# Joined q/k rest rows, score groups merged per half, and a mode preference in the order, on a TensorE-bound four-layer attention kernel

## The chip, the core and the metric

The kernel runs on one core of a Trainium2 chip. The metric is the device time of one execution in microseconds (us). Runs of one kernel spread by 3 to 17 us, so small differences are compared only between kernels that ran beside each other.

## The reference

Four residual layers run over 2048 rows of 576 values. Layers of kind A are local attention (32 heads of 18, a window of 8 with stride 2). Layers of kind B are a recurrence over 64 segments of 32 rows: each segment attends, with 32 heads of 128, over 8 memory rows and itself, and its first 8 output rows are the next memory.

```
for s in range(n_seg):                                   # layer B, cut
    h = concatenate([mem, x[:, s*32:(s+1)*32]])          # 8 + 32 rows of 576
    q, k, v = h @ Wq, h @ Wk, h @ Wv                     # 32 heads of 128
    p = softmax(mask(q @ k.T * 128**-0.5))
    o = (p @ v) @ Wo
    mem = o[:, :8]; outs.append(o[:, 8:])
x = x + A(layernorm(x)); x = x + B(layernorm(x))         # and both once more
```

## The kernel before

Both B layers run at once as two "lanes", the second five segments behind. So a step has 80 columns (two segments of 32, two memories of 8); the first and last five of the 69 steps have one lane. The A layers' tiles fill TensorE between. A small planner in Python lays out all operations at build time: each has an engine, a duration, a priority and buffers, and at each free moment the ready operation of lowest priority number is emitted. The order on the chip is fixed from then on.

```
# q and k of 3 heads (cut): ten matmuls a head, the fifth of each over the last 64 of 576 rows
for wi in range(2):
    for kc in range(4):
        matmul(pv[:, hh, wi, a:b], lhsT=wt[:, kc, h*P:(h+1)*P], rhs=hT[:, kc, a:b], start=(kc == 0), stop=False)
    matmul(pv[:, hh, wi, a:b], lhsT=wr[:, (h%16)*P:(h%16+1)*P], rhs=hT[:, 4 + h//16, a:b], start=False, stop=True)
...
# scores of 16 heads, called once with kind "m" (memory) and once with "x"
matmul(v, lhsT=ident4, rhs=msk, start=True)              # the mask, 128*128 tile
for l in lanes: for i in range(4): for c in range(4):    # 128*32 tiles, four side by side
    matmul(v[c*32:(c+1)*32, ...], lhsT=q, rhs=k)
...
# the planner's choice (cut)
while heap:
    it = heapq.heappop(heap); o = it[2]
    ...
    if all buffers of o are free:
        pick = o
        break
    skipped.append(it)
```

TensorE takes a tile shape per matmul; 128*128 is the whole array, 128*32 one of four column strips, 32*128 one of four row strips.

## Time and profile before

| | before |
|---|---|
| time, median of 3 runs | 2204.92 us (2199.17 to 2209.19) |
| span of the profiled run | 2198.3 us, TensorE clock 0.993 |
| TensorE matmul busy / weight loads busy | 95% / 79% |
| matmuls | 62,649 |
| largest groups | L818 and L820 (q and k), L974 (output projection), L864 (v) |

The page's first part gives busy time by engine, the fourth the chain of work that ended last. How the two are read together stands at the head of the prediction.

### The profile page before, as it was taken

To read this page: it belongs to the slowest core of one execution; us is meant where nothing else is said; L and a number is where in the kernel's file an instruction comes from. 1 tells how busy PE (TensorE), PEld (TensorE's weight loads), DVE (VectorE), ACT (ScalarE), POOL (GpSimd) and SP (SyncE) were. 2 spreads that over 40 slices of the span, in tenths; PEclk is the share of its full clock that TensorE was granted. 3 is DMA by queue.
4 is the path that set the end of the run, shared out by engine and by line. 5 is a ranking of instruction groups with operands and counts; after the bars stand their busy time and mean duration, and the time that the engine had idled before them with its cause. 6 is when DMAs were issued, how large, how long until landed. Compare 5 with 4: busy or idle time off the path is not lost.

```text
span 2198.3 us, 136770 instructions
## 1 busy us (share of the span) xinstructions
PE 2094.2 (95%) x62649; PEld 1746.3 (79%) x62649; DVE 1438.0 (65%) x3599; ACT 1189.0 (54%) x2855; POOL 853.9 (39%) x1263
## 2 busy tenths in 40 slices
PE   2689999999999999999999999999999999999998
PEld 2577888888888888888888888878878888888876
DVE  4467676666667666666766676667667666765665
ACT  2345565555556555555555565555555555655544
POOL 4144433443444344344434433443343344333230
PEclk9799999999999999999999999999999999999999
DMA  9754343343343334334433343443334333432210
GB/s 286 219 163 137 119 122 110 116 138 111 111 130 120 114 117 129 121 106 133 123 107 118 123 129 112 120 123 115 111 123 129 112 120 123 122 101 80 71 57 10
DMA packets 158578, 265.39 MB, mean 121 GB/s; under 512 B 23592, under 2 KB 90032, under 8 KB 158000
## 3 DMA queue, kind: packets, MB, share of 16 engines
q1 hardware_dynamic: 153168, 237.77, 35.2%
q0 software_dynamic: 4832, 18.88, 2.6%
q8 instruction: 489, 8.01, 1.5%
q14 instruction: 89, 0.73, 0.1%
HBM read 240.46 MB, written 16.12 MB: 117 GB/s over the span
## 4 chain that ended last, share of the span: by engine, by line
PE 87%; DMA 8%; DVE 2%; issue 1%; POOL 0%; ACT 0%; SPq 0%; POOLq 0%; ACTq 0%; DVEq 0%
PE r L818 28%; PE r L974 17%; PE r L864 14%; PE r L557 7%; PE r L820 7%; DMA ring<-strip 6%; PE r L909 3%; PE r L897 3%; PE r L950 2%; PE r L667 2%; PE r L458 2%; PE r L631 1%; PE r L606 1%; DMA ring<-in_A_wqkv_dram 1%; DMA wo<-in_A_wo_dram 1%
## 5 line engine op out<-in xcount | busy, mean ns | idle before, releaser
L818 PE MATMUL r<-hT,wq 128*128 128x80 bf16 (+1 forms) x8832 | 667.8, 199 | 4.4 <-ACT hT L268 2.8
L818 PE MATMUL r<-hT,wk 128*128 128x80 bf16 (+1 forms) x8832 | 666.0, 199 | 0.1
L268 ACT ACTIVATE qk<-r 128x480 bf16<-128x480 f32 (+3 forms) x714 | 379.5, 532 | 285.7 <-PE r L820 251.5
L818 PEld LDWEIGHTS <-wq 128*128 128x128 bf16 x8832 | 443.4, 99 | 57.8 <-issue 44.2
L818 PEld LDWEIGHTS <-wk 128*128 128x128 bf16 x8832 | 447.5, 100 | 0.2 <-issue 0.2
L974 PE MATMUL r<-OT,wo 128*128 128x80 bf16 (+1 forms) x11040 | 423.4, 199 | 22.7 <-issue 15.1
L820 PE MATMUL r<-hT,wk_r 128*128 128x80 bf16 (+1 forms) x2208 | 439.2, 199 | 0.2 <-issue 0.2
L820 PE MATMUL r<-hT,wq_r 128*128 128x80 bf16 (+1 forms) x2208 | 439.2, 199 | 0.0
L974 PEld LDWEIGHTS <-wo 128*128 128x128 bf16 x11040 | 398.3, 99 | 32.8 <-issue 30.0
L275 POOL TENSOR_TENSOR big<-qT,kT 128x1024 bf16<-128x1024 bf16 x189 | 319.1, 1691 | 213.4 <-ACT kT L268 206.7
L864 PE MATMUL r<-wv,hT 128*32 128x512 bf16 x5376 | 351.9, 380 | 1.4 <-issue 1.4
L275 POOL TENSOR_TENSOR ex<-ex,sum 128x384 bf16<-128x384 bf16 x137 | 120.3, 878 | 557.3 <-ACT qk L268 396.9
L864 PEld LDWEIGHTS <-hT 128*32 128x32 bf16 x6720 | 166.5, 96 | 134.8 <-issue 2.2
L755 DVE TENSOR_REDUCE nmx<-r 128x4 f32<-128x320 f32 (+1 forms) x276 | 143.5, 520 | 184.3 <-PE r L909 183.1
L268 ACT ACTIVATE V<-r 128x512 bf16<-128x512 f32 x302 | 180.2, 597 | 114.8 <-PE r L864 106.4
L557 PE MATMUL r<-xn,ring 128*128 128x64 bf16 x4725 | 192.8, 194 | 28.9 <-DMA ring<-in_A_wqkv_dram 17.3
L820 PEld LDWEIGHTS <-wq_r 128*128 128x128 bf16 x2208 | 219.8, 100 | 0.0
L820 PEld LDWEIGHTS <-wk_r 128*128 128x128 bf16 x2208 | 219.7, 100 | 0.0
L557 PEld LDWEIGHTS <-ring 128*128 128x128 bf16 x4725 | 159.8, 98 | 45.9 <-DMA ring<-in_A_wqkv_dram 18.2
L270 DVE CAST big<-r 128x256 bf16<-128x256 f32 x255 | 112.9, 484 | 93.7 <-PE r L631 92.8
L275 POOL TENSOR_TENSOR big<-big 128x640 bf16<-128x640 bf16 (+1 forms) x34 | 50.0, 1470 | 315.5 <-DVE big L275 315.4
L268 ACT ACTIVATE OT<-r 128x320 bf16<-128x320 f32 (+1 forms) x350 | 125.9, 421 | 54.8 <-PE r L950 54.3
(148 smaller groups left out, 3186.3 us busy)
## 6 DMA issues: line engine op xcount, KB each, us to landing
ring<-strip SPq DMA_DIRECT2D x488, 320.0 KB, 3.4
ring<-strip SPq DMA_DIRECT2D x244, 160.0 KB, 4.0
x1T<-x SPq DMA_DIRECT2D x32, 160.0 KB, 4.2
x<-x1T SPq DMA_DIRECT2D x32, 160.0 KB, 4.2
x3T<-x SPq DMA_DIRECT2D x32, 160.0 KB, 4.2
x<-x3T SPq DMA_DIRECT2D x32, 160.0 KB, 3.9
wo<-in_B_Wo_dram POOLq DMA_DIRECT2D x4, 1152.0 KB, 10.5
wq<-in_B_Wq_dram POOLq DMA_DIRECT2D x4, 1024.0 KB, 11.0
```

The lines of the kernel that those rows point to most:

```text
L268: nc.scalar.activation(out=out, in_=in_, func=ACT.Copy, scale=1.0 if scale is None else scale)
L270: (nc.vector if e == "DVE" else nc.gpsimd).tensor_copy(out=out, in_=in_)
L275: (self.nc.vector if e == "DVE" else self.nc.gpsimd).tensor_tensor(out=out, in0=in0, in1=in1, op=op)
L458: nc.tensor.matmul(psf, lhsT=(self.ones if c < 4 else self.ones_h)[:, :], rhs=xs.t[:, c].rearrange("p a t -> p (a t)"), start=(c == 0), st ...
L557: nc.tensor.matmul(ps.t[:, c * T:(c + 1) * T], lhsT=view()[:, kc, w0:w0 + P], rhs=xn.t[:, kc, :], start=(kc == 0), stop=(kc == 4))
L755: nc.vector.tensor_reduce(out=m, in_=v, axis=AX.X, op=ALU.max, negate=True)
L818: nc.tensor.matmul(pv[:, hh, wi, a:b], lhsT=wt[:, kc, h * P:(h + 1) * P], rhs=hT.t[:, kc, a:b], start=(kc == 0), stop=False)
L820: nc.tensor.matmul(pv[:, hh, wi, a:b], lhsT=wr[:, (h % 16) * P:(h % 16 + 1) * P], rhs=hT.t[:, 4 + h // 16, a:b], start=False, stop=True)
L864: nc.tensor.matmul(ps.t[c * 32:(c + 1) * 32, :], lhsT=l, rhs=w, start=(kc == 0), stop=(kc == 4))
L897: nc.tensor.matmul(v, lhsT=self.ident4[:], rhs=msk, start=True, stop=False, skip_group_check=True)
L909: nc.tensor.matmul(out, lhsT=q_, rhs=k_, start=False, stop=True, skip_group_check=True)
L974: nc.tensor.matmul(psY.t[:, mb * W80 + c0:mb * W80 + c1], lhsT=self.wo[:, w0:w0 + P], rhs=self.OT[:, h % 16 // 4 * 8 + h // 16 * 4 + h % 4 ...
```

## The change

Three things were meant. The last 64 input rows of q and of k become one matmul: their weights lie one above the other in 128 partitions, and the moving operand has, as it already had, the rest rows once in the upper and once in the lower half with zeros elsewhere (block-diagonal), so that 160 columns give q's and k's share. The memory and x scores of a half are one operation with both masks first, to change the tile shape less often. And the planner prefers an operation of the mode that TensorE is in. New priorities come with it.

```diff
+                        if alt is not None and o.prio > alt.prio + PR["w"]:
+                            skipped.append(it)
+                            break
 ...
-                            pick = o
-                            break
+                            if e != "PE" or o.mode == mode:
+                                pick = o
+                                break
+                            if alt is None:
+                                alt = o
 ...
-                    nc.tensor.matmul(pv[:, hh, wi, a:b], lhsT=wr[:, (h % 16) * P:(h % 16 + 1) * P],
-                                     rhs=hT.t[:, 4 + h // 16, a:b], start=False, stop=True)
+                nc.tensor.matmul(pv[:, hh, :, a:b], lhsT=self.Wb[0][1][:, h * P:(h + 1) * P], rhs=hT.t[:, 4:6, a:b],
+                                 start=False, stop=(hh == n - 1), skip_group_check=True)
 ...
-    def scores(self, t, r, kind, prio):
+    def scores(self, t, r, prio):
+            for v, msk in ((m, mask_m), (x, mask_x)):        # shortened here
+                nc.tensor.matmul(v, lhsT=self.ident4[:], rhs=msk, start=True, stop=False, skip_group_check=True)
+            # then 16 memory scores, then 16 a lane of x scores
 ...
-PR = dict(qk=0.218, qkd=0.046, v1=1.418, v0=1.316, m0=-0.184, x0=-0.028, m1=-0.12, x1=-0.059, ...
+PR = dict(qk=0.388, qkd=0.053, v1=1.358, v0=0.674, w=-0.059, s0=0.051, s1=-1.024, ...
```

More of the change, by code (lines that the diff above doesn't have):

```diff
@@ L153, in run @@
                     skipped = []
-                    pick = None
+                    pick = alt = None
                     held = set()
@@ L170, in run @@
                         if all(len(self.pools[p]) >= k and p not in held for p, k in need.items()):
-                            pick = o
-                            break
-                        if HOLD:
+                            if e != "PE" or o.mode == mode:
[3 more added lines that the diff above has]
+                                alt = o
+                        elif HOLD:
                             held.update(p for p, k in need.items() if k > 1 and len(self.pools[p]) < k)
@@ L177, in run @@
                         heapq.heappush(heap, it)
-                    if pick is None:
+                    if pick is None and alt is None:
                         continue
+                    pick = pick or alt
                     o = pick
@@ L336, in setup @@
         self.Wb = []
+        qkr = cp.tile([P, NH * P], BF16, name="wqk_r")
         for nm in ("wq", "wk", "wv"):
-            self.Wb.append((cp.tile([P, 4, NH * P], BF16, name=nm), cp.tile([P, (NH // 2) * P], BF16, name=nm + "_r")))
+            self.Wb.append((cp.tile([P, 4, NH * P], BF16, name=nm), cp.tile([P, (NH // 2) * P], BF16, name="wv_r") if nm == "wv" else qkr))
         self.wo = wo = cp.tile([P, NH * D + 64], BF16, name="wo")
@@ L416, in prologue @@
                 for hf in range(2):
-                    o = load(wr[hf * 64:(hf + 1) * 64, :], src[i][512:576, hf * 16:(hf + 1) * 16].rearrange("p h e -> p (h e)"), 0.26)
+                    if i < 2:
+                        out, in_ = wr[i * 64:(i + 1) * 64, hf * 16 * P:(hf + 1) * 16 * P], src[i][512:576, hf * 16:(hf + 1) * 16]
+                    else:
+                        out, in_ = wr[hf * 64:(hf + 1) * 64, :], src[i][512:576, hf * 16:(hf + 1) * 16]
+                    o = load(out, in_.rearrange("p h e -> p (h e)"), 0.26)
             for n in range(4):
@@ L815, in mm @@
                 for wi in range(2):
-                    wt, wr = self.Wb[wi]
                     for kc in range(4):
-                        nc.tensor.matmul(pv[:, hh, wi, a:b], lhsT=wt[:, kc, h * P:(h + 1) * P], rhs=hT.t[:, kc, a:b],
-                                         start=(kc == 0), stop=False)
-                    nc.tensor.matmul(pv[:, hh, wi, a:b], lhsT=wr[:, (h % 16) * P:(h % 16 + 1) * P],
-                                     rhs=hT.t[:, 4 + h // 16, a:b], start=False, stop=True)
-        o = pl.op("PE", 0.0003 + (0.358 if b - a == W80 else 0.29) * n, mm, prio, [*self.x_in[t].values(), *self.mem_in[t]] + ([self.w_in[wi][n_] for wi in range(2) for n_ in
-                  {h // 8 for h in heads}] if t == 0 else []), acq=[ps, sb], uses=[hT], mm=10 * n)
+                        nc.tensor.matmul(pv[:, hh, wi, a:b], lhsT=self.Wb[wi][0][:, kc, h * P:(h + 1) * P], rhs=hT.t[:, kc, a:b],
+                                         start=(hh == 0 and wi == 0 and kc == 0), stop=False, skip_group_check=True)
+                nc.tensor.matmul(pv[:, hh, :, a:b], lhsT=self.Wb[0][1][:, h * P:(h + 1) * P], rhs=hT.t[:, 4:6, a:b],
+                                 start=False, stop=(hh == n - 1), skip_group_check=True)
+        o = pl.op("PE", 0.0003 + (0.356 if b - a == W80 else 0.275) * n, mm, prio, [*self.x_in[t].values(), *self.mem_in[t]] + ([self.w_in[wi][n_] for wi in range(2) for n_ in
+                  {h // 8 for h in heads}] if t == 0 else []), acq=[ps, sb], uses=[hT], mm=9 * n)
         if g == 0:
@@ L874, in scores, with vm, vx @@
         qkt = dict(self.qkt)
-        ps = pl.buf("r")
-        m = kind == "m"
-        e_ = pl.buf("e" + kind)
-        pt, after = (pl.buf("pt"), None) if m else self.PT[r]
+        psm, psx, em, ex, pt = pl.buf("r"), pl.buf("r"), pl.buf("em"), pl.buf("ex"), pl.buf("pt")
         k0 = 16 * (1 - t % 2)
         on = self.lanes(t)
-        self.e_[kind] = e_
-        def view(tile_):
-            return tile_[:, 0:320].rearrange("p (i k) -> p i k", i=4) if m else \
-                tile_[:, 0:384].rearrange("p (l i k) -> p l i k", l=2, i=4)
+        def vm(tile_):
+            return tile_[:, 0:320].rearrange("p (i k) -> p i k", i=4)
+        def vx(tile_):
+            return tile_[:, 0:384].rearrange("p (l i k) -> p l i k", l=2, i=4)
         def mm(e):
-            v = view(ps.t)
+            m, x = vm(psm.t), vx(psx.t)
             def q(h, a, n):
@@ L894, in k @@
                 return qkt[h // 3].t[:, h % 3, 1, a:a + n]
-            msk = self.mask_m[:].unsqueeze(1).to_broadcast([P, 4, W80]) if m else \
-                self.mask_x[:].unsqueeze(2).to_broadcast([P, 2, 4, 48])
-            nc.tensor.matmul(v, lhsT=self.ident4[:], rhs=msk, start=True, stop=False,
-                             skip_group_check=True)
-            for l in range(1 if m else 2):
-                if not m and not on[l]:
-                    continue
+            for v, msk in ((m, self.mask_m[:].unsqueeze(1).to_broadcast([P, 4, W80])),
+                           (x, self.mask_x[:].unsqueeze(2).to_broadcast([P, 2, 4, 48]))):
+                nc.tensor.matmul(v, lhsT=self.ident4[:], rhs=msk, start=True, stop=False, skip_group_check=True)
@@ L902, in mm @@
+            for i in range(4):
+                for c in range(4):
+                    h = heads[i][c]
+                    nc.tensor.matmul(m[c * 32:(c + 1) * 32, i, :], lhsT=q(h, MC, 32), rhs=k(h, 0, W80), start=False, stop=True,
+                                     skip_group_check=True)
+            for l in range(2):
                 for i in range(4):
-                    for c in range(4):
+                    for c in range(4 if on[l] else 0):
                         h = heads[i][c]
-                        if m:
-                            out, q_, k_ = v[c * 32:(c + 1) * 32, i, :], q(h, MC, 32), k(h, 0, W80)
-                        else:
-                            out, q_, k_ = v[c * 32:(c + 1) * 32, l, i, :], q(h, XC[l], 32), k(h, KX[l], 48)
-                        nc.tensor.matmul(out, lhsT=q_, rhs=k_, start=False, stop=True, skip_group_check=True)
@@ L910, in scores @@
-        o = pl.op("PE", 0.29 if m else 0.41 if all(on) else 0.29, mm, prio, [self.qk_ev[g] for g in gs], acq=[ps, e_], uses=[qkt[g] for g in gs], mode="C",
-                  mm=17 if m or not all(on) else 33)
-        if m:
-            o = self.softmax(t, ps, e_, 320, prio, o, "DVE", view, lambda x: x[:, :, 16:96], lambda x: x[:, :, k0:k0 + 96],
-                             lambda x: x[:, :, :, MC:MC + 32], 384, pt, True)
-        else:
-            def tout(x):
-                f = x[:, 0, 0, 0:1]
-                return bass.AP(f.tensor, f.offset, [list(f.ap[0]), [W80 + XC[1], 2], [3 * W80, 4], [W80, 2], [1, 32]])
-            o = self.softmax(t, ps, e_, 384, prio + 0.02, o, "POOL", view, lambda x: x[:, :, :, 16:64],
-                             lambda x: x[:, :, :, k0:k0 + 64].rearrange("p l i (b q) -> p l i b q", q=32), tout, 512, pt, False, after)
@@ L922, in scores @@
-        self.PT[r] = (pt, o)
+                        nc.tensor.matmul(x[c * 32:(c + 1) * 32, l, i, :], lhsT=q(h, XC[l], 32), rhs=k(h, KX[l], 48), start=False,
+                                         stop=True, skip_group_check=True)
+        o = pl.op("PE", 0.68 if all(on) else 0.56, mm, prio, [self.qk_ev[g] for g in gs], acq=[psm, psx, em, ex],
+                  uses=[qkt[g] for g in gs], mode="C", mm=50 if all(on) else 34)
+        a = self.softmax(t, psm, em, 320, prio, o, "DVE", vm, lambda x: x[:, :, 16:96], lambda x: x[:, :, k0:k0 + 96],
+                         lambda x: x[:, :, :, MC:MC + 32], 384, pt, True)
@@ L924, in vs, with tout @@
+        def tout(x):
+            f = x[:, 0, 0, 0:1]
+            return bass.AP(f.tensor, f.offset, [list(f.ap[0]), [W80 + XC[1], 2], [3 * W80, 4], [W80, 2], [1, 32]])
+        a = self.softmax(t, psx, ex, 384, prio + 0.02, o, "POOL", vx, lambda x: x[:, :, :, 16:64],
+                         lambda x: x[:, :, :, k0:k0 + 64].rearrange("p l i (b q) -> p l i b q", q=32), tout, 512, pt, False, a)
+        self.PT[r] = (pt, a)
     def vs(self, t):
@@ L1024, in b_step @@
         for r in range(2):
-            self.scores(t, r, "m", t + PR[f"m{r}"])
-            self.scores(t, r, "x", t + PR[f"x{r}"])
+            self.scores(t, r, t + PR[f"s{r}"])
         for r in range(2):
@@ L1075 @@
 DLY = 5
-PR = dict(qk=0.218, qkd=0.046, v1=1.418, v0=1.316, m0=-0.184, x0=-0.028, m1=-0.12, x1=-0.059, p0=1.154, p1=-0.868,
-          o=0.742, od=0.026, mo=0.874, xo=0.964, v2=2.065, a1=1.97, a1s=2.63, a2=0.983, a2s=2.137, fin=1.091,
-          res=-1.854, ring=-7.995, A=(0.197, 0.389, 1.2, 0.915, 0.033, 1.069, 0.267, 1.19))
+PR = dict(qk=0.388, qkd=0.053, v1=1.358, v0=0.674, w=-0.059, s0=0.051, s1=-1.024, p0=0.894, p1=-0.981, o=0.434,
+          od=0.001, mo=0.097, xo=1.092, v2=2.128, a1=2.228, a1s=1.274, a2=0.453, a2s=7.821, fin=6.362, res=-5.467,
+          ring=-6.659, A=(-0.104, 0.482, 0.742, 0.737, 0.843, -0.012, 0.929, 0.994))
 LEAD = 5
```

## The prediction

> **What bounds the kernel now.** I read the busy shares first, then the chain that ended last, then the waits of TensorE, then the timeline of a stretch in the middle.
>
> ```profile
> PE 2094.2 (95%) x62649; PEld 1746.3 (79%) x62649; DVE 1438.0 (65%) x3599; ACT 1189.0 (54%) x2855; POOL 853.9 (39%) x1263
> ...
> PE 87%; DMA 8%; DVE 2%; issue 1%; POOL 0%; ACT 0%; SPq 0%; POOLq 0%; ACTq 0%; DVEq 0%
> PE r L818 28%; PE r L974 17%; PE r L864 14%; PE r L557 7%; PE r L820 7%; DMA ring<-strip 6%; PE r L909 3%; PE r L897 3%; PE r L950 2%; PE r L667 2%; PE r L458 2%; PE r L631 1%; PE r L606 1%; DMA ring<-in_A_wqkv_dram 1%; DMA wo<-in_A_wo_dram 1%
> ```
>
> TensorE is the bound: 95% busy, 87% of the last chain, the next engine at 65%. Busy does not say what a matmul costs, since consecutive matmuls overlap (one "takes" 202 ns in the groups while the next begins 36 ns later). Costs must come from start to start. The waits that TensorE itself suffered are small:
>
> ```profile
> PE r L557 <- DMA ring<-in_A_wqkv_dram: 17.3, 4, 12.0
> PE r L974 <- issue: 15.1, 20, 2.3
> PE r L557 <- DMA ring<-strip: 11.1, 23, 1.7
> ```
>
> The first is the start-up, which the stretches show too: of the first 100 us TensorE is busy 44.54, from 1000 to 2000 us it is busy 985.11. "issue" is 20 halts in which nothing visible is waited for. In the instruction records they recur at one position modulo 256 instructions (drifting slowly from 178 to 124), about 1.4 us after a 16 KiB packet of the instruction queue has ended: TensorE has run past what was fetched. I count some 20 us of these.
>
> So time is TensorE's stream: the start-to-start intervals of 62,649 matmuls. In the timeline (start, duration):
>
> ```profile
> 1015.41 0.20 PE L820 MATMUL r<-hT,wk_r 128*128 128x80 bf16 x1
> 1015.45 0.31 PE L818 MATMUL r<-hT,wq 128*128 128x80 bf16 x4
> 1015.59 0.20 PE L820 MATMUL r<-hT,wq_r 128*128 128x80 bf16 x1
> 1015.62 0.31 PE L818 MATMUL r<-hT,wk 128*128 128x80 bf16 x4
> ...
> 1023.92 0.39 PE L864 MATMUL r<-wv_r,hT 128*32 128x512 bf16 x4
> 1024.24 0.31 PE L897 MATMUL r<-mask_m,ident 128*128 128x320 bf16 x1
> 1024.48 0.33 PE L909 MATMUL r<-qk 128*32 128x80 bf16 x16
> 1024.74 0.34 PE L897 MATMUL r<-mask_x,ident 128*128 128x384 bf16 x1
> 1025.01 0.38 PE L909 MATMUL r<-qk 128*32 128x48 bf16 x32
> 1025.32 0.90 PE L557 MATMUL r<-xn,ring 128*128 128x64 bf16 x25
> ```
>
> Five matmuls of 80 columns take 1015.45 to 1015.62: 0.18 us, 36 ns each. Their record starts give 35.8 ns. One score pair (both halves of 16 heads) changes the tile shape four times, mask (128*128) to scores (128*32) and back, and takes 1024.24 to 1025.32, 1.08 us.
>
> **What the Trainium skill says.** "TensorE: Matmul & The Clock Gate", section "Wait — 56ns, not 53.3ns?", gives a warm matmul N/2.4 + about 2.5 ns from start to start, and a floor near 25 ns. The trace agrees: 35.8 ns at N = 80 (formula 35.8), 29 at 64 (29.2), 56 at 128 (55.8), 25 at 40 columns. "TensorEngine Tiling (Array Packing)", section "Key Properties", says that changing the tiling mode drains TensorE. The trace agrees and gives the price: after an 80-column full-array matmul the next starts 36 ns later in the same shape and 132 to 134 later in another; after a 512-column 128*32 group 206 against 312; after the 320-column mask 232 to 239 against 136 by the formula. About 0.10 us per change, in each direction. "Runtime: NRT & Kernel Launch", section "Instruction fetch mechanics", has instructions refilled in blocks of 16 KiB, 256 instructions; the halts at one position modulo 256 agree, but they are not "mostly hidden" here.
>
> **The change, part by part.**
>
> *q and k rest rows.* Ten matmuls a head become nine: two of 80 columns become one of 160. The same columns stream, so only the fixed cost of one matmul goes: 2 x 35.8 - (160/2.4 + 2.5 = 69.2) = 2.5 ns, an estimate by the page's formula. There are 1888 such heads (59 steps of both lanes x 32): 4.7 us. In the ten one-lane steps 2 matmuls at 40 columns, at the floor (25 to 26 ns), become one of 80: 51.2 - 35.8 = 15.4 ns x 320 heads = 4.9 us. Together 9.6 us, not the 156 us which 2208 x 2 x 35.8 ns of L820 might suggest. 2208 weight loads go too; loading overlaps and is no bound at 79%.
>
> *Merged scores.* Both masks first, then both score blocks: one change into the score shape instead of two, and one out. That is 138 pairs x up to 2. Reading the two builds' TensorE orders, changes of shape fall from 1423 to 1156: mask to scores from 276 to 138, and scores to something of another shape from 206 to 40 (98 groups now run straight into a v pass of the same 128*32 shape, where 70 did). 267 x 0.10 = 26.7 us.
>
> *Preference for the current mode.* As built it does nothing. The constant w is -0.059, and candidates come in rising priority, so once a ready operation of another mode is kept as alternative, the next has a priority above it minus 0.059 and ends the search at once. Building the changed kernel with the preference taken out gives the same order on all five engines. What remains of that part is the new set of priorities, and that reorders everything.
>
> Stream total: 9.6 + 26.7 = 36 us. As a cross-check I priced every neighbouring pair of both orders with the median (or trimmed mean) start-to-start of the same kind of pair in the trace: 2057 us before, 2018 after, 39 less. All of it is TensorE time, on the path.
>
> *What the new order gives back.* The work between a producer on TensorE and its consumer shrinks in places. In every second step the first output projection now follows its attention-times-V block after only ten 64-column transposes, 0.58 us by those same prices; the trace shows 0.79 us from last such matmul through the ScalarE eviction (0.44 us) to the first projection. So 0.2 us x some 30 = 6 us come back. Second: before, memory scores were done some 0.5 us ahead of x scores; now both reach VectorE at once, so the x softmax starts about that much later. Measured from scores to the last transpose it took 5.6 to 6.2 us, the new gap is 6.6 to 6.8 us: just enough, or short by 0.1 us. I take 2 us for that. The gap from the last projection to the next step's q and k is as before (1.25 us).
>
> Sum: 2204.9 - 36 + 8 = 2177; with half of what the pricing of pairs finds beyond the two terms, and some chance that re-chosen priorities also trim existing waits, I put 2172.
>
> **The rivals.**
>
> *Instruction fetch becomes the wait.* A group of 50 score matmuls is 100 instructions in some 0.9 us. Against: the group lies beside v passes (27 ns per instruction), and nine matmuls a head stretch 18 instructions over 355 ns (19.8 ns each instead of 17.9). Summing 320-instruction stretches, the new order is no denser. If fetch halts doubled: 2190.
>
> *Softmax or PSUM becomes the wait.* A score group now needs two PSUM banks of eight and both exponent buffers at once, and the burst lands on VectorE together. If each half waited 0.3 us more (138 x 0.3 = 41 us), the whole gain would go: about 2210. Against: VectorE 65%, and the attention block of the first half comes over 11 us after its scores.
>
> *Everything lands, with fewer waits.* If also half of the roughly 2 us per 100 us of waits in the middle vanish: about 2150, past the 2% mark of 2160.8.
>
> **Range and chances.** The stream saving is firm within some 4 us, what the order gives back is uncertain by 15, and single runs of before spread by 10. Range 2150 to 2194. Faster by over 2%: 0.24; within 2%: 0.73; slower: 0.03.
>
> **What would show it.** Matmuls 62,649 to 60,441; a 160-column matmul 69 ns before its successor; mask_m to mask_x 136 ns and no scores between; a two-step period in the middle down from 63.8 us to about 62.8. Waits of TensorE for OT before L984 of 0.2 us every second step. I am wrong if the 160-column matmul, whose operand lies in two pieces, streams slower than one per column, if pt becomes a frequent releaser of TensorE, or if "issue" grows well past 20 us.

## The result, and the profile after

The changed kernel takes 2169.28 us (median of 4, 2168.33 to 2171.51) against 2207.06 for before beside it (the three runs above and one more). The ratio is 0.9835 (95% interval 0.9805 to 0.9864), a gain of less than 2%. A ratio is the mean time of one kernel's runs over that of the other's of the same rounds, so not quite the ratio of the medians quoted.

The same parts of the page for the changed kernel, engines and chain:

```profile
PE 2063.7 (95%) x60441; PEld 1727.7 (80%) x60441; DVE 1397.7 (64%) x3541; ACT 1157.2 (53%) x2838; POOL 939.7 (43%) x1338
...
PE 90%; DMA 5%; DVE 2%; issue 1%; ACT 1%; POOL 1%; SPq 0%; POOLq 0%; ACTq 0%; DVEq 0%
```

TensorE is the bound as before, at the same 95%, and its share of the chain has risen. The matmuls are the 60,441 expected. The shares alone would not tell that the kernel is faster.

TensorE's own waits (who waited for whom: total us, times, longest):

```profile
PE r L533 <- DMA x<-in_A_x_dram: 25.0, 1, 25.0
PE r L570 <- DMA ring<-in_A_wqkv_dram: 16.0, 8, 7.4
...
PE r L984 <- issue: 7.4, 20, 0.9
...
PE r L570 <- DMA ring<-strip: 2.4, 6, 0.6
```

The first line is new: one wait of 25 us for one small input load. The second is the start-up's, about as before (17.3); "issue" at the output projection is down from 15.1, though halts elsewhere make up for it (below). The last was 11.1 us before and is 2.4. One score group in the middle of the run, in the timeline (start, duration):

```profile
1011.44 0.39 PE L877 MATMUL r<-wv_r,hT 128*32 128x512 bf16 x4
1011.76 0.31 PE L909 MATMUL r<-mask_m,ident 128*128 128x320 bf16 x1
1011.91 0.33 PE L909 MATMUL r<-mask_x,ident 128*128 128x384 bf16 x1
1012.16 0.33 PE L913 MATMUL r<-qk 128*32 128x80 bf16 x16
1012.32 0.43 PE L919 MATMUL r<-qk 128*32 128x48 bf16 x32
1012.57 1.06 PE L877 MATMUL r<-wv,hT 128*32 128x512 bf16 x16
```

From the first mask to what follows it is 0.81 us where it was 1.08. Those 1.08 us ended in one more change of shape, though. The like of it before is a group that a v pass followed:

```profile
1015.80 0.30 PE L897 MATMUL r<-mask_m,ident 128*128 128x320 bf16 x1
1016.03 0.33 PE L909 MATMUL r<-qk 128*32 128x80 bf16 x16
1016.29 0.34 PE L897 MATMUL r<-mask_x,ident 128*128 128x384 bf16 x1
1016.56 0.38 PE L909 MATMUL r<-qk 128*32 128x48 bf16 x32
1016.78 1.06 PE L864 MATMUL r<-wv,hT 128*32 128x512 bf16 x16
```

It took 0.98 us, so merging alone saves 0.17 here, two changes of shape. In the changed kernel the second mask starts 0.15 us after the first, no drain between, and the v pass after the scores has their shape, so nothing is drained there either, as in the group just shown.

To see where the time went I cut the run at the first output projection of steps 15 and 55, and sorted the start-to-start intervals of all matmuls in the middle stretch. An interval more than 60 ns above the median of its kind of pair counts as a "wait" if the matmul or its weight load carries a semaphore wait, and as a "halt" if not; "rest" is the stream. A short wait that recurs at the same pair stays in the rest.

| us | first matmul to step 15 | step 15 to 55 | of it halts | waits | rest | step 55 to last matmul |
|---|---|---|---|---|---|---|
| before | 542.0 | 1274.8 | 14.3 | 12.2 | 1248.4 | 367.7 |
| after | 540.3 | 1250.5 | 15.0 | 1.0 | 1234.5 | 363.2 |
| change | -1.7 | -24.3 | +0.7 | -11.2 | -13.9 | -4.5 |

So of 30.5 us in these two traces, 24.3 came in the middle 40 steps, a little more than half of it as a shorter stream and nearly half as waits that are gone. The first 15 steps gave almost nothing. The waits went with the new order: the same count gives 17.6 us of them in e6_before_qk below, which keeps the old order, and 0.7 to 2.2 us in the ten traces that have the new one (all but e5_pref and e7_oldprio). No run has the new order with the operations of before, so what the new priorities do without the merging is not known.

### The profile page after: what moved, and what is told of

Same layout as the page of the kernel before. It is cut to its first block, busy times and chain, and to the rows that moved or that the text cites. A ratio compares the mean times of both kernels' runs of the same rounds, so it can differ in the third digit from the quotient of the medians.

```text
span 2167.8 us, 132202 instructions
## 1 busy us (share of the span) xinstructions
PE 2063.7 (95%) x60441; PEld 1727.7 (80%) x60441; DVE 1397.7 (64%) x3541; ACT 1157.2 (53%) x2838; POOL 939.7 (43%) x1338
## 4 chain that ended last, share of the span: by engine, by line
PE 90%; DMA 5%; DVE 2%; issue 1%; ACT 1%; POOL 1%; SPq 0%; POOLq 0%; ACTq 0%; DVEq 0%
PE r L830 27%; PE r L984 18%; PE r L877 17%; PE r L570 7%; PE r L833 6%; PE r L960 3%; PE r L680 2%; PE r L909 2%; DMA ring<-strip 2%; PE r L471 2%; DMA ring<-in_A_wqkv_dram 2%; PE r L913 2%; PE r L644 1%; PE r L919 1%; PE r L619 1%
## 5 line engine op out<-in xcount | busy, mean ns | idle before, releaser
L830 PEld LDWEIGHTS <-wq 128*128 128x128 bf16 x8832 | 500.7, 98 | 31.6 <-issue 21.5
L833 PE MATMUL r<-hT,wqk_r 128*128 128x160 bf16 (+1 forms) x2208 | 507.9, 230 | 0.1
L275 ACT ACTIVATE qk<-r 128x480 bf16<-128x480 f32 (+3 forms) x635 | 333.2, 525 | 238.0 <-PE r L833 225.0
L282 POOL TENSOR_TENSOR big<-qT,kT 128x1024 bf16<-128x1024 bf16 x186 | 310.1, 1686 | 32.7 <-ACT kT L275 21.5
L282 POOL TENSOR_TENSOR big<-big 128x640 bf16<-128x640 bf16 (+1 forms) x59 | 117.6, 1994 | 414.7 <-ACT xs L465 245.0
L833 PEld LDWEIGHTS <-wqk_r 128*128 128x128 bf16 x2208 | 219.5, 99 | 0.2 <-issue 0.2
L570 PEld LDWEIGHTS <-ring 128*128 128x128 bf16 x4725 | 160.9, 98 | 42.7 <-DMA ring<-in_A_wqkv_dram 17.6
L275 ACT ACTIVATE OT<-r 128x320 bf16<-128x320 f32 (+1 forms) x377 | 138.3, 425 | 103.6 <-PE r L960 103.3
L275 ACT ACTIVATE big<-r 128x384 bf16<-128x384 f32 (+1 forms) x290 | 110.3, 443 | 92.8 <-issue 67.6
L769 DVE TENSOR_TENSOR r<-r,nmx 128x320 f32<-128x320 f32 (+1 forms) x276 | 147.1, 533 | 9.4
L877 PE MATMUL r<-wv_r,hT 128*32 128x512 bf16 x1344 | 133.2, 379 | 0.0
```

The lines of the kernel that those rows point to most:

```text
L275: nc.scalar.activation(out=out, in_=in_, func=ACT.Copy, scale=1.0 if scale is None else scale)
L282: (self.nc.vector if e == "DVE" else self.nc.gpsimd).tensor_tensor(out=out, in0=in0, in1=in1, op=op)
L570: nc.tensor.matmul(ps.t[:, c * T:(c + 1) * T], lhsT=view()[:, kc, w0:w0 + P], rhs=xn.t[:, kc, :], start=(kc == 0), stop=(kc == 4))
L769: nc.vector.tensor_tensor(out=v, in0=v, in1=m.unsqueeze(len(shp) - 1).to_broadcast(shp), op=ALU.add)
L830: nc.tensor.matmul(pv[:, hh, wi, a:b], lhsT=self.Wb[wi][0][:, kc, h * P:(h + 1) * P], rhs=hT.t[:, kc, a:b], start=(hh == 0 and wi == 0 and ...
L833: nc.tensor.matmul(pv[:, hh, :, a:b], lhsT=self.Wb[0][1][:, h * P:(h + 1) * P], rhs=hT.t[:, 4:6, a:b], start=False, stop=(hh == n - 1), sk ...
```

## The experiments

Each kernel is the changed one with the edit shown, unless it says before. "Rest", "halts" and "waits" are those of the table, in the middle 40 steps of the profiled run. The four kernels from a0_after to e3_tiled ran beside each other, so did e4_x1early to e7_oldprio, and so did a1_after to e9_cond_x1.

**a0_after and a1_after: the controls.** No edit.

> The changed kernel again, as the control for the three runs beside it: 2169 us as on record, ratio to before 0.9835. Nothing is tested by it alone.

> The changed kernel again, control for the three runs beside it: 2170 to 2172 us.

Measured: 2171.56 us (ratio 0.9812) and 2175.59 us (0.9829). The rest is 1234.5 us in both and in the trace on record, the same to 0.1 us, while halts run from 15.0 to 17.0 and the time up to step 15 from 540.3 to 549.2. So the stream repeats exactly, and what differs between runs of one kernel lies in halts and the start-up.

**e1_split: the join undone, the order kept.**

```diff
-                nc.tensor.matmul(pv[:, hh, :, a:b], lhsT=..., rhs=hT.t[:, 4:6, a:b], ...)
+                for wi in range(2):
+                    nc.tensor.matmul(pv[:, hh, wi, a:b], lhsT=..., rhs=hT.t[:, 4 + wi, a:b], ...)
```

> The changed kernel with the joined rest-row matmul taken apart again into two (80 columns each, or 40), the order of every engine left as it is. My theory (only the fixed 2.5 ns of a matmul goes in the wide steps, 15 ns a head in the one-lane steps): 9.6 us slower than the control, so about 2179. Rival: the join was worth nothing, because the operand in two pieces costs the 2.5 ns again (the records show 71.6 ns to the next matmul, not 69.2): about 5 us slower, from the one-lane steps alone. Rival: fewer instructions also spared fetch halts: 15 us or more slower, with issue waits of TensorE clearly up.

Measured: 2183.96 us (0.987), 12.4 above its control. The rest rises by 3.0 us (1237.5), which over the 1280 heads of the stretch is 2.3 ns a head; halts are 15.5 against 16.8. So the join is worth what was worked out, some 2.3 x 1888 = 4.4 us in the wide steps and about 5 in the one-lane ones; the remaining 3 us of the 12.4 have no cause shown; single runs of either kernel spread by 3.5 to 8. The record that alarmed me, 71.6 ns from a joined matmul to the next, is undone by its neighbours: the other 80-column intervals in the same heads average 35.5 ns in place of 35.8. A single interval was a bad witness, the sum over a head a good one. The fetch rival (15 us or more, with more halts) falls: 4416 instructions more brought no more halts in this stretch.

**e2_apart: the x mask back between the score blocks, all else in place.**

```diff
-  mask_m, mask_x, memory scores, x scores
+  mask_m, memory scores, mask_x, x scores
```

> The changed kernel with the same operations in the same order, but inside each of the 138 score groups the mask of the x scores is put back between the two score blocks: changes of tile shape go from 1156 to 1432. My theory (0.10 us a change, all on the path): 276 x 0.10 = 28 us slower than the control, about 2197. Rival (what the switches cost is hidden behind waits that follow): under 10 us slower. The memory scores are then ready earlier by about 0.35 us, which would show if the softmax were on the path.

Measured: 2193.08 us (0.991), 21.5 above its control. The rest rises by 14.2 us (1248.7) for 160 more changes of shape in the stretch: 0.089 us a change. So shape changes are on the path and nearly as dear as priced. 276 changes at 0.089 would be 24.6 us, where 21.5 was measured. Halts are 13.1 us, 3.7 fewer than in the control. A slower group may give the fetch more time, but that is not shown: the halts of other pairs with the same middle differ by as much (e8_tiled_x1).

**e3_tiled: masks as strips of the scores' own shape.**

```diff
-                nc.tensor.matmul(v, lhsT=self.ident4[:], rhs=msk, start=True, stop=False, skip_group_check=True)
+                for c in range(4):
+                    nc.tensor.matmul(v[c * 32:(c + 1) * 32], lhsT=self.ident4[:, c * 32:(c + 1) * 32], rhs=msk, start=True, ...)
```

> The changed kernel with each mask written by four 128*32 matmuls (one per column strip) in place of one 128*128, so that a score group is of one tile shape from its first instruction: shape changes from 1156 to 966, matmuls up by 828. My theory: 190 x 0.10 = 19 us faster than the control, about 2150, if four strips stream beside each other as the v passes do (206 ns for four of 512 columns). Rival: the strips go one after another, 2 x 3 more streams of 133 to 160 ns, and it is 40 us slower or worse. Rival: the group, now 112 instructions in a burst, brings fetch halts: gain under 8 us with issue waits up.

Measured: 2164.53 us (0.9782), 7.0 below its control. The same kind of place in its timeline:

```profile
1001.61 0.39 PE L877 MATMUL r<-wv_r,hT 128*32 128x512 bf16 x4
1001.83 0.31 PE L910 MATMUL r<-mask_m,ident 128*32 128x320 bf16 x4
1001.96 0.34 PE L910 MATMUL r<-mask_x,ident 128*32 128x384 bf16 x4
1002.13 0.32 PE L915 MATMUL r<-qk 128*32 128x80 bf16 x16
```

From the last v block to the memory scores it is 0.52 us, where the changed kernel has 1011.44 to 1012.16, 0.72. The strips do stream side by side (0.13 us to the next four), and the first rival falls. The rest is 13.1 us less for 120 fewer changes, 0.109 us each. But halts rise by 4.3 (21.1 against 16.8), which would fit the second rival; e8_tiled_x1 below puts that in doubt. The middle says -7.8 us in all, the time -7.0.

**e4_x1early and e4b_x1early: the second input tile's load first.** The line with the 25 us wait above has its cause in the queue of the SyncE transfers (start, duration):

```profile
10.04 0.35 SPq L443 DMA_DIRECT2D x<-in_B_mem_dram  x1
...
22.93 5.92 SPq L505 DMA_DIRECT2D wo<-in_A_wo_dram  x1
28.95 20.13 SPq L528 DMA_DIRECT2D x<-in_A_x_dram  x2
```

There is one buffer for input rows. The start memory takes it at 10 us, and the second tile's load, now of a lower rank, stands behind all the strips of A's weights, to be issued at 28.95 and to land some 19 us later among the B weights. Before, and again in e4b_x1early, it is issued at 10 us:

```profile
10.03 0.47 SPq L515 DMA_DIRECT2D x<-in_A_x_dram  x1
10.04 0.47 SPq L528 DMA_DIRECT2D x<-in_A_x_dram  x1
```

The edit:

```diff
-                      pr(0), [dep], acq=[x0])
+                      -2.6 if j == 1 else pr(0), [dep], acq=[x0])
```

> The changed kernel with one priority altered: the load of the second input tile goes ahead of the load of the start memory, as it did before the change; the steady order stays. My theory (the re-chosen priorities put that load behind the big weight loads, TensorE waited 25 us for it, and the first q and k came 17.7 us later, of which all but about 7 us was caught up within ten steps): first q and k at about 46 us again, and 7 us faster than the changed kernel, about 2162. Rival: nothing is caught up, 17 us faster. Rival: the start is bound by the weights anyway, within 2 us.

> The kernel of e4_x1early once more, now beside its control, since without one the gain read as anything from 8 to 13 us. Theory (late start, mostly caught up within ten steps): 7 to 10 us below the control. Rival (nothing caught up): 17 us below.

Measured: 2163.06 us (0.9777), and beside its control 2163.50 (0.9772), 12.1 below it, more than the 7 to 10 expected and less than 17. The first q and k start at 46.5 us (52.8 in the second trace) where the changed kernel has 63.6 and before 45.8. The expected 7 to 10 rested on one trace: there those 17.7 us of delay, set against before, had shrunk to 6.4 by step 5 and 0.6 by step 10. The two controls still had 8.8 and 12.0 at step 5, 5.2 and 8.7 at step 10. At step 15 the three traces of the changed kernel stand on average 2.7 us behind before (from 1.7 ahead to 7.1 behind), the two with the early load 6.0 and 7.1 ahead of it. So the late start is caught up in part only: about 9 us of it stay, in traces that differ by as much among themselves. Before, TensorE was busy only 44.54 of the first 100 us, so a late start has idle time to catch up in. So the new priorities brought a late start that costs the changed kernel about 12 us by the time measured, 9 by the traces.

**e5_pref: the preference turned on.**

```diff
-PR = dict(..., w=-0.059, ...
+PR = dict(..., w=0.3, ...
```

> The changed kernel with the preference for the current tile mode truly on (w = 0.3 in place of -0.059), all other priorities as they are: shape changes from 1156 to 1004. If switches alone counted: 152 x 0.10 = 15 us faster, about 2154. My theory: the order was chosen for w = -0.059, and work of one mode held together delays producers (attention blocks pushed to three in a row, then all projections), so TensorE waits more than it gains: 2160 to 2220, with PE waits for OT, pt or DMA up.

Measured: 2256.64 us (1.0208), some 85 us above the changed kernel, beyond my range. Shape changes are fewer (580 in the stretch against 680), waits 38.1 us against 1.0, and the start is longer too (571.7 us to step 15). For 88.7 us of that start the granted clock was at half, against 14 to 68 in the changed kernel's three traces, so a part of the longer start may be the clock. Of TensorE's waits over the whole run:

```profile
PE r L570 <- DMA ring<-strip: 16.8, 30, 1.1
PE r L728 <- DVE fin L1023: 12.7, 27, 0.6
```

The changed kernel had 2.4 and 0.4 us there. A preference that saves 0.1 us a time delays work whose consumers then wait. This shows what w = 0.3 does with priorities chosen without it, not that no preference could pay.

**e6_before_qk: before, with the join alone, its order kept.** The edit is the rest-row part of the diff of the change (the `matmul` lines), with the weight tile that it needs.

> The kernel before with only the joined rest-row matmul, its order on every engine kept (1423 shape changes). My theory: 9 to 10 us faster than before, ratio 0.9957. Rival: under 3 us, the join is hidden. Rival: over 20 us, because 4416 fewer TensorE instructions spare fetch halts.

Measured: 2197.55 us (0.9942, interval 0.9915 to 0.9968), 12.6 below before. The rest is 3.6 us less (1244.8), 2.8 ns a head. Its profiled run was the slowest of its six (2209.68). Together with e1_split: the join gives about 10 us in either order, 12.4 and 12.6 in time and 9.6 as worked out.

**e7_oldprio: the change with the priorities of before.**

```diff
-PR = dict(qk=0.388, ..., s0=0.051, s1=-1.024, ...
+PR = dict(qk=0.218, ..., s0=-0.184, s1=-0.12, ...
```

> The changed kernel with the priorities of before (score groups at the old priority of the memory scores): joined matmul and merged groups without the new priorities. Shape changes 975, fewer than the 1156 of the changed kernel, so by switches alone it should be 18 us faster than the changed kernel, about 2150. My theory: the priorities were chosen for another set of operations, waits come up in the middle (TensorE busy under 985 of 1000 us), and it is slower than the changed kernel: 2170 to 2230. What it is above 2170 is what the new priorities are worth.

Measured: 2443.05 us (1.1053), far beyond my range, although it changes shape less often than the changed kernel (560 times in the stretch against 680). Where TensorE waited:

```profile
PE r L570 <- DMA ring<-strip: 71.5, 82, 3.2
PE r L471 <- ACT xs L465: 44.7, 30, 1.5
PE r L984 <- ACT OT L275: 36.0, 68, 0.6
```

Waits in the stretch are 69.8 us, and the rest is up by 133, which holds short waits that recur, and slower matmuls: the granted clock from 600 to 1800 us is 0.95. The trace's clock records tell how: of the stretch's 1443.7 us, 140 were at half clock, some 7 us in every 72 (before and after had none there). In them 80-column matmuls followed each other after 66.7 ns in place of 35.6. That makes some 65 of the 133 us, an estimate from these figures. All four runs had 0.944 to 0.953, so it belongs to this kernel, but what brought the clock down is not shown. So join and merging together did not pay under the old priorities: 270 us slower than under the new ones, the clock's share included. How the two depend on each other in detail is not settled by this run.

**e8_tiled_x1: strips and the early load.** The edits of e3_tiled and e4_x1early.

> The early load of the second input tile together with the masks as 128*32 strips. If the two are independent: 7 (strips, as in e3_tiled) + 9 (load) = 16 us below the control, about 2155. Rival: less than 12, if the fetch halts that ate most of the strips' gain grow.

Measured: 2153.88 us (0.973), 21.7 below its control, where 16 were expected: 12.1 from the load and 9.6 from the strips on top of it. Rest 1221.4 as in e3_tiled, halts 17.5 where e3_tiled had 21.1. The order in the middle is the same in both; the start differs. So how many halts a kernel gets varies by some 4 us for reasons outside the burst itself, and the single figure of e3_tiled should not be leaned on.

**e9_cond_x1: strips only after a 128*32 block.**

```diff
+                        self.was = mode                                  # in the planner
 ...
+                if pl.was != "C":
+                    nc.tensor.matmul(v, lhsT=self.ident4[:], rhs=msk, start=True, ...)
+                    continue
```

> As e8_tiled_x1, but a group that follows a full-array matmul keeps its two full-array masks; only the 95 or so groups that follow a 128*32 block use strips. Shape changes as in e8_tiled_x1 (966), 258 matmuls fewer. If fetch halts are what took most of the strips' gain in e3_tiled, a shorter burst gives some back: 1 to 3 us below e8_tiled_x1, with issue waits down. If not: the same as e8_tiled_x1 within 1 us.

Measured: 2147.35 us (0.9704, interval 0.9691 to 0.9717), 28.2 below its control and 6.5 below e8_tiled_x1. This is the fastest kernel and correct; it beats before and after. Why it beats e8_tiled_x1 is open. The reason I gave is not borne out: halts in its profiled run are 22.2 against 17.5, the rest is the same 1221.4, and the two profiled runs differ by only 1.6 us (spans 2148.9 and 2150.5), while the timed medians differ by 6.5.

## Why the prediction was right

The predicted 2172 stands against 2169.28, inside the range of 2150 to 2194 and within 2%, to which it had given 0.73. The direction, the bound and the main mechanisms held. Not every term did. Of the signs it named, the matmul count and the two-step period came (63.7 to 62.5 us, where 62.8 was expected); the two short intervals came a little longer (71.6 ns after a 160-column matmul for 69, 143.5 from mask to mask for 136).

*Rest rows, 9.6 us.* Right: 2.3 to 2.8 ns a head in the wide steps by the rest of e1_split and e6_before_qk, where 2.5 was worked out; 12.4 and 12.6 us in time, some 3 us more than was worked out. (The 156 us of L820 that the prediction sets beside it should be 158; no sum uses it.)

*Merged scores, 26.7 us at 0.10 a change.* The mechanism is right, the size about a tenth too large. A change costs 0.089 us in e2_apart and 0.109 in e3_tiled, so 0.10 is fair for the stream. But in the middle 160 changes went (840 to 680) and the rest fell by 13.9 us, of which 3.0 belong to the join: 10.9 us, 0.068 each. Most of the difference is the give-back that the prediction counted apart: the 0.17 us of the next paragraph but one, which recur, sit in the rest. In this stretch there are 19 of them, 3.4 us; without them it is 14.3 us, 0.089 each, as in e2_apart. That other small differences between the two orders come to nothing is not shown: the pricing of pairs had 19.3 us for that stretch, join included, where 13.9 and 3.4 make 17.3.

*The preference does nothing.* Right, and lucky for the kernel: turned on with these priorities it costs 85 us.

*What the order gives back, 6 us for the projection.* Right in place: 26 times the first projection stands after the transposes (five of them turned out to be 128 columns wide, of finished rows) with an interval 0.17 us over its usual, 4.5 us in all; from attention block to projection it is 0.73 us where 0.58 was priced. *2 us for the later softmax*: wrong, nothing. TensorE waits for pt 5.8 us in six places in all, none of them from 600 to 1800 us.

*The rivals.* Fetch as the new wait: no, halts 14.3 to 15.0. Softmax or PSUM: no. Fewer waits: yes. I gave "half of the 2 us per 100 us" only as a rival that would end at 2150. That figure held halts too: waits and halts of the middle made 26.5 us before, 2.1 per 100 us, and 16.0 after, so 40% of it went, all of it waits (12.2 to 1.0).

*The halts.* That they recur at one position modulo 256 is right, and plainer than it was read. Counted over matmuls and weight loads alone, in order of start, the position does not drift: all 31 halts over 0.3 us of before (whole run) and all 39 of after stand at 193 to 195. The instruction queue moved 489 packets in before, and its 125,298 matmuls and weight loads over 256 are 489.4. So the fetch is well supported as their cause; no run changed it alone.

*What was missed.* The start: the new priorities moved one input load behind the weights, about 12 us by e4b_x1early. I had looked at the order of TensorE and not at that of the transfers, where one line would have shown it. The two missed terms, 11 us of waits gone and about 12 us at the start, nearly cancel. The closeness of the total owes something to that, and that much was luck.

## What to carry to other kernels

When one engine's stream is the bound, price it from start to start by kind of neighbour pair: joining two matmuls of 80 columns saved only some 2.5 ns, because the same columns stream, while a change of tile shape costs about 0.1 us here, as much as three matmuls of 80 columns. Look for instructions that could take the shape of their neighbours (the masks as strips gave 7.0 and 9.6 us). An order chosen for one set of operations has to be chosen anew when they change, with its start-up and its transfer queues read too.

## What the Trainium skill lacked or had wrong

- "TensorEngine Tiling (Array Packing)", section "Key Properties", says that a change of mode drains TensorE and gives no price. Here it is 0.089 us (14.2 us for 160 changes, e2_apart) to 0.109 us (13.1 us for 120, e3_tiled).
- "Runtime: NRT & Kernel Launch", section "Instruction fetch mechanics", calls the cost of crossing a 16 KiB boundary mostly hidden. In a TensorE stream of short matmuls it shows: 31 halts of 14.3 us together in 1274.8 us before, 48 of 22.2 us in 1245.6 in the fastest kernel, the long ones all at one position modulo 256 instructions.
- "TensorE: Matmul & The Clock Gate", section "Wait — 56ns, not 53.3ns?", N/2.4 + 2.5 ns: held in sums for an operand of two pieces of 80 columns (2.3 ns saved a head, e1_split). Single record intervals do not follow it there: 71.6 ns after the joined matmul where the formula has 69.2, with the neighbouring ones shorter by 0.3 ns.
